# Top-k attention, convolution gate and phase mixer on one core: bringing 1 / sum to the columns of x by products with the identity

## The chip, the cores and the metric

One NeuronCore of a Trainium2 chip runs the whole program. The metric is the device time in microseconds (us) of that core; a lower time is better. The engines that compute are TensorE (PE; its weight loads have a row of their own, PEld), VectorE (DVE), ScalarE (ACT) and GpSimd (POOL). SyncE (SP) issues most of the DMAs.

## The reference

Three blocks follow each other. The first is attention that keeps the 32 largest scores of a row; the second multiplies a convolution gate by a projection; the third mixes phases over tokens and channels. Cut to what matters here:

```python
scores = scale * np.matmul(q, k.transpose(0, 1, 3, 2))          # batch 4, heads 8, 576 x 576, head size 64
kth = np.partition(scores, -32, axis=-1)[..., -32:-31]
scores = np.where(scores >= kth, scores, -1e9)
attn = np.exp(scores - scores.max(-1, keepdims=True))
attn = attn / (attn.sum(-1, keepdims=True) + 1e-09)              # 1 / sum: what the change is about
x = np.matmul(attn, v)                                           # then (batch, 576, 512)

gate_pre = causal_conv5(x, conv_w);  x = (sigmoid(gate_pre) * (x @ w_val)) @ w_out

theta = x @ w_theta
y = w_tok_r @ (x * cos(theta)) + w_tok_i @ (x * sin(theta));  u = x + y
out = u + np.maximum(u @ w_ch, 0.0)
```

## The kernel before

The 32 heads are 16 units `u` of two heads `j` each, four units to a batch. The 576 queries of a head are tiles of 128 rows; the last 64 rows of both heads share one tile. That gives 9 tiles a unit, 144 in all. A tile belongs to a part `(u, x)`: part 0 holds the first 256 columns of x (4 tiles), part 1 the other 320 (5 tiles). Batch 0 takes all its parts 0 first and then all its parts 1 (`SPLIT`); the other batches go unit by unit.

The main loop (L1321) runs one step `i` per tile and writes out the order of the work by hand. In step `i` the kernel computes the scores of tile `i + 3` on PE (`scores_pe`), takes the scores of tile `i + 2` out of PSUM with ACT (`scores_out`), picks the largest of tile `i` on DVE (`pick`, six MAX8 of L573), masks tile `i - 6` (L656) and turns and copies tile `i - 7` (`turn`, `turn_out`). ACT and DVE keep exactly that order; PE, POOL and SP are ordered by priority, which mostly follows it.

When the last tile of a part has been masked, `close` starts a chain (L690). It is a generator that is advanced twice in a step, before `turn` and at the step's end. Call the step in which it starts T. It adds 1e-9 to the row sums (POOL) and takes the reciprocal `rs` (DVE). The sums stand one to a partition, but x is computed with heads and features on partitions and queries in columns, so 1 / sum has to be brought to columns. Before, this takes two hops: `rows` transposes `rs` on PE, and ACT copies the result to `rT` (4 or 5 rows); then `columns(0)` and `columns(1)` multiply a row of the identity by `rT`, and ACT copies each result into `rb`. Meanwhile the products `px` of probabilities and values (L749) run into one of the four buffers of `ps_m`, the PSUM pool that the other two blocks use too. At last DVE multiplies `px` by `rb` (L767), which frees that buffer.

Small PE work that needs some PSUM columns waits in the list `extras`: `last_rows` of every tile (L672, 128 columns, put first), `rows` (128), `columns` (128 or 192). `scores_pe` fills it into the columns that scores leave free: 256 in the bank of the first 256 scores, 192 in the bank of the other 320. Its ACT copies follow the two evictions of that tile in the next step (`run(follow)`).

The last two blocks are jobs (`front`, `back`) that `work` feeds to PE in each step, up to a planned 4150 ns (`BASE`, L63), in order of batches. `front(b)` is appended behind the multiply L767 of the batch's last unit. `drain(("gate", ...))` (L775) runs jobs at once, without the budget, until the gate tiles of an earlier batch are free; the fifth unit before the current one names that batch.

The heads of a unit are loaded by `load_heads`, split into a high and a low half by ACT (`split_high`, L238) and POOL (`split_low`, L244), and copied to where scores use them by `double`. The tuple `when` (L1228) says in which steps this happens: 9, 8, 7, 6 and 3 steps before the unit's first tile, or 7, 5, 5, 4 and 3 steps before it in batch 0. Unit 4 is the first unit of batch 1; its first tile is tile 36, and the part before it, `(3, 1)`, has its first tile at 31. All the loads land in single buffers (`kl`, `ql`).

Of the kernel before, what the change touches and what calls it, by code (L numbers as in the profile page):

```python
# [11 lines left out]
F32 = mybir.dt.float32  # L12
# [29 lines left out]
SPLIT = (0,)  # L42
# [50 lines left out]
def mixer(ctx, tc, qT, kT, vt, w_val, conv_t, w_out, w_theta, w_tok, w_ch, out, flag):  # L93
    nc = tc.nc
    safe = flag is None
    P = 128
    B, S, DM = vt.shape
    U = qT.shape[0]
    NP = U // B
    H2 = S // 2  # L100
    NF = S // P
    REM = S - NF * P
# [418 lines left out]
    def scores_pe(i):  # L521

        s_psum[i] = []
        for lo, hi in COLS:
# [14 lines left out]
            while extras and extras[0][0] <= 512 - a:  # L539
                c, on_pe = extras.pop(0)  # L540
                follow.append(on_pe(bank[:, a : a + c]))
                a += c
# [147 lines left out]
    def close(part):  # L690
# [7 lines left out]
        rT = wk.tile([5, P], F32, tag="rT", name=f"rT_{u}_{x}")  # L698
# [3 lines left out]
        done = set()  # L702

        def rows(spare):
            nc.tensor.transpose(spare[:n, :P], rs[:, :n], ident)

            def f():
                nc.scalar.copy(rT[:n], spare[:n, :P])
                done.add("rows")
            return f  # L710

        def row(k):
            return ident[:n, k : k + 1].broadcast_to([n, 64])

        def columns(m):


            def on_pe(spare):
                c = P + REM * (m * x)
                for j in range(2):  # L720
                    r = slice(64 * j, 64 * j + 64)
                    nc.tensor.matmul(spare[r, :P], row(2 * j + m), rT[:n], start=True, stop=True,  # L722
                                     skip_group_check=True)
                    if c > P:
                        nc.tensor.matmul(spare[r, P:c], row(4), rT[:n, r], start=True, stop=True,
                                         skip_group_check=True)

                def f():
                    nc.scalar.copy(rb[:, m * P : m * P + c], spare[:, :c])  # L729
                    done.add(m)  # L730
                return f
            return on_pe

        extras.append((P, rows))
        yield
        yield
        asked = "rows" in done
        if asked:
            extras.extend((P + REM * (x * m), columns(m)) for m in range(2))
# [17 lines left out]
        while "rows" not in done:  # L757
            yield
            yield
        if not asked:  # L760
            extras.extend((P + REM * (x * m), columns(m)) for m in range(2))
        yield
        yield
        while 1 not in done:
            yield
            yield
# [610 lines left out]
```

## Time and profile before

| what | before |
|---|---|
| time, median of 3 runs | 872.44 us (871.95 to 874.28) |
| profiled execution: its time, its span | 878.3 us, 876.5 us |
| PE busy | 757.3 us (86%) |
| DVE busy | 725.9 us (83%) |
| ACT busy | 652.3 us (74%) |
| POOL busy | 409.2 us (47%) |
| mean granted TensorE clock | 0.932 |

A profile is one execution. Busy times say how much work an engine has; what delays the end is read from idle times and from what ended them. In a line of a timeline the columns are start, duration, engine, line and operation, the tiles written and read, the shape, how many instructions are merged, and in brackets the idle time before the first of them and who ended it.

### The profile page before, as it was taken

What the parts mean: (1) busy time and instruction counts of PE and PEld (TensorE: products, weight loads), DVE (VectorE), ACT (ScalarE), POOL (GpSimd) and SP (SyncE); (2) the same over time, 40 slices, a digit from 0 to 9 for tenths busy, and PEclk for the clock granted to TensorE, in tenths of its full rate; (3) what the DMA queues carried; (4) which work ended last, traced back from release to release, by engine and by line L of the source; (5) the groups of instructions that cost most, each with busy time, mean ns of one, the idle gap of its engine ahead of it and who ended that gap; (6) DMA issues with size and microseconds to landing.
All of it is one profiled execution on the core that took longest, in us unless ns stands there. A gap on an engine that the chain in (4) does not pass through costs nothing.

```text
span 876.5 us, 15920 instructions
## 1 busy us (share of the span) xinstructions
PE 757.3 (86%) x4526; PEld 575.6 (66%) x4526; DVE 725.9 (83%) x2952; ACT 652.3 (74%) x1591; POOL 409.2 (47%) x435
## 2 busy tenths in 40 slices
PE   4477876947879689989798999999998999999995
PEld 2344554624556358676678577769697776699895
DVE  5999998879999778989999999899988697444522
ACT  5787896878979587687878898798987895445611
POOL 4655555344555324354758634445677233003700
PEclk9996788966899979999899999999999999999998
DMA  5665555613433124324735552132755110042001
GB/s 148 169 183 166 143 141 152 174 48 92 131 92 93 43 67 128 94 55 114 225 112 185 191 163 61 46 94 58 216 135 154 44 67 15 1 155 93 3 1 58
DMA packets 73601, 94.35 MB, mean 108 GB/s; under 512 B 13728, under 2 KB 37152, under 8 KB 73504
## 3 DMA queue, kind: packets, MB, share of 16 engines
q1 hardware_dynamic: 73184, 92.82, 37.6%
q8 instruction: 38, 0.62, 0.3%
q14 instruction: 59, 0.48, 0.2%
q10 hardware_dynamic: 320, 0.43, 0.1%
HBM read 49.96 MB, written 13.11 MB: 72 GB/s over the span
## 4 chain that ended last, share of the span: by engine, by line
PE 41%; DVE 37%; ACT 11%; issue 5%; DMA 2%; POOL 2%; SPq 1%; ACTq 0%; POOLq 0%; DVEq 0%
PE py L1090 8%; DVE cand L573 8%; PE px L749 8%; DVE tops L598 6%; DVE s L656 5%; PE ph L507 4%; PE pval L507 3%; DVE cand L579 3%; PE pt L669 3%; PE py L1109 3%; DVE tops L577 3%; PE px2t L507 3%; DVE gp L804 3%; PE ps L536 2%; PE pth L507 2%
## 5 line engine op out<-in xcount | busy, mean ns | idle before, releaser
L593 POOL TENSOR_TENSOR y<-s,n 128x576 f32<-128x576 f32 x144 | 188.4, 1308 | 199.5 <-DVE tops L598 101.6
L573 DVE MAX8 cand<-s 128x8 f32<-128x96 f32 x864 | 210.8, 245 | 1.4 <-ACT s L550 1.4
L585 ACT ACTIVATE n<-s,tops 128x576 bf16<-128x576 f32 x144 | 112.0, 778 | 50.3 <-DVE tops L577 34.4
L656 DVE SCALAR_TENSOR_TENSOR s<-s,thrs,e 128x576 f32<-128x576 f32 x144 | 137.9, 958 | 5.7 <-ACT e L193 5.7
L669 PE MATMUL pt<-ident,s 128*128 128x128 f32 x576 | 99.0, 296 | 49.3 <-ACT pT L688 34.5
L550 ACT ACTIVATE s<-ps 128x256 f32<-128x256 f32 (+1 forms) x288 | 103.9, 406 | 38.2 <-PE ps L722 15.0
L669 PEld LDWEIGHTS pt<-ident,s 128*128 128x128 f32 x576 | 71.1, 149 | 78.1 <-ACT pT L688 42.6
L1090 PE MATMUL py<-w_tok,z 128*128 128x256 f32 (+1 forms) x432 | 115.6, 410 | 6.9 <-DVE z L949 6.7
L749 PE MATMUL px<-pT,v 128*64 128x256 f32 (+3 forms) x640 | 113.3, 455 | 8.2 <-ACT pT L688 7.2
L598 DVE MAX8 tops<-y 128x8 f32<-128x576 f32 x144 | 108.0, 750 | 11.7 <-POOL y L593 11.7
L193 ACT ACTIVATE e<-s,least 128x576 f32<-128x576 f32 x144 | 110.5, 768 | 1.3 <-DVE s L656 0.9
L536 PE MATMUL ps<-kh_None,q 128*128 128x256 f32 x240 | 96.9, 410 | 5.9 <-ACT rb L729 2.7
L688 ACT COPY pT<-pt 128x512 f32<-128x512 f32 x128 | 73.2, 571 | 29.1 <-PE px L749 14.7
L1090 PEld LDWEIGHTS py<-w_tok,z 128*128 128x128 f32 x432 | 78.4, 191 | 24.8 <-issue 7.3
L749 PEld LDWEIGHTS px<-pT,v 128*64 128x64 f32 (+1 forms) x640 | 46.1, 148 | 58.8 <-issue 30.9
L577 DVE MAX8 tops<-cand 128x8 f32<-128x48 f32 x432 | 82.9, 192 | 0.1
L537 PE MATMUL ps<-kl_None,q 128*128 128x256 f32 x240 | 73.7, 309 | 0.0
L536 PEld LDWEIGHTS ps<-kh_None,q 128*128 128x128 f32 x240 | 48.5, 202 | 26.9 <-ACT s L550 7.5
L536 PE MATMUL ps<-kh,q 128*128 128x256 f32 (+1 forms) x80 | 40.1, 506 | 20.5 <-ACT s L550 11.4
L579 DVE MATCH_REPLACE8 cand<-tops,cand 128x48 f32<-128x48 f32 x288 | 55.3, 192 | 0.0
L804 DVE SCALAR_TENSOR_TENSOR gp<-xT,w_conv,gp 128x576 f32<-128x576 f32 (+2 forms) x60 | 50.1, 836 | 4.7 <-POOL gp L796 4.0
L537 PEld LDWEIGHTS ps<-kl_None,q 128*128 128x128 f32 x240 | 49.1, 205 | 3.4 <-issue 1.6
(208 smaller groups left out, 1695.7 us busy)
## 6 DMA issues: line engine op xcount, KB each, us to landing
kh_None<-kh_None SPq DMA_DIRECT2D x48, 144.0 KB, 2.5
kl_None<-kl_None SPq DMA_DIRECT2D x48, 144.0 KB, 2.6
v<-in_vt_dram SPq DMA_DIRECT2D x20, 256.0 KB, 2.9
out_dram<-x2T SPq DMA_DIRECT2D x16, 256.0 KB, 3.2
w<-ch SPq DMA_DIRECT2D x16, 256.0 KB, 4.3
w<-theta SPq DMA_DIRECT2D x16, 256.0 KB, 5.5
raw_hi<-in_w_tok_dram SPq DMA_DIRECT2D x14, 256.0 KB, 2.9
kh<-kh SPq DMA_DIRECT2D x24, 144.0 KB, 2.4
```

Of the source, the lines that this page charges most:

```text
L193: ins = nc.scalar.activation(out, src, func, **more).ins
L536: nc.tensor.matmul(bank[:, :w], q2, kh[:, lo:hi], start=(j == js[0]), stop=False)
L537: nc.tensor.matmul(bank[:, :w], q2, kl[:, lo:hi], start=False, stop=(j == js[-1]))
L573: nc.vector.max(d["cand"][:, k, 8 * x : 8 * x + 8], s_tiles[i][:, x * SUB : (x + 1) * SUB])
L577: nc.vector.max(top, c)
L585: nc.scalar.activation(n, s_tiles[i], AF.Sign, bias=d["tops"][:, k, KC - 1 : KC], scale=-(1.0 + 2.0 ** -22), accum_out=d["acc"][:, k : k + 1])
L593: nc.gpsimd.tensor_tensor(y, s_tiles[i], d.pop(("n", k)), ALU.mult)
L598: nc.vector.max(d["tops"][:, k, KC:K], d.pop(("y", k)))
L656: nc.vector.scalar_tensor_tensor(p, p, thrs[:, i : i + 1], e.exp, ALU.is_ge, ALU.mult, accum_out=part["sums"][:, e.slot : e.slot + 1])
L669: nc.tensor.transpose(e.pt[:, c, :], p[:, c * P : (c + 1) * P], ident)
L749: nc.tensor.matmul(px[64 * j : 64 * j + 64, :], v[r, c, 64 * j : 64 * j + 64], pT[r, k, :], start=(c == 0), stop=(c == NF), skip_group_che ...
L1090: nc.tensor.matmul(ps, z[:, m * P : (m + 1) * P], W["tok"][:, w, lo:hi], start=(i + k == 0), stop=(i == NF))
```

## The change

1. `rs` is brought to columns in one hop. `blocks` makes four products: the stationary operand is a column of `rs`, broadcast to 64, and the moving operand is the identity. They fill 256 columns of one bank, and one ACT copy takes them to `rb`. For part 1, `rows` makes two more products of 64 rows and 64 columns and one more small copy. The transpose, `rT` and the two copies of `columns` are gone.
2. The chain asks for these products at the end of step T, and multiplies from step T + 3 on.
3. `extras` is no longer taken in order: the bank of the first 256 scores takes only items of more than 128 columns (`blocks`), the other bank all the rest (`last_rows`, `rows`).
4. The steps of `when` for unit 4 become 7, 5, 5, 4 and 3 before its first tile.

```diff
-            while extras and extras[0][0] <= 512 - a:
-                c, on_pe = extras.pop(0)
+            for item in list(extras):
+                c, on_pe = item
+                if c > 512 - a or (lo == 0) != (c > P):
+                    continue
+                extras.remove(item)
                 follow.append(on_pe(bank[:, a : a + c]))
                 a += c
...
+        def blocks(spare):
+            for m in range(2):
+                for j in range(2):
+                    nc.tensor.matmul(spare[64 * j : 64 * j + 64, m * P : m * P + P],
+                                     rs[:, 2 * j + m : 2 * j + m + 1].broadcast_to([P, 64]), ident,
+                                     start=True, stop=True, skip_group_check=True)
+            def f():
+                nc.scalar.copy(rb[:, : 2 * P], spare)
+                spread.add(0)
+            return f
         def rows(spare):
-            nc.tensor.transpose(spare[:n, :P], rs[:, :n], ident)
+            for j in range(2):
+                r = slice(64 * j, 64 * j + 64)
+                nc.tensor.matmul(spare[r, :], rs[r, 4:5].broadcast_to([64, 64]), ident[r, r],
+                                 start=True, stop=True, skip_group_check=True)
             def f():
-                nc.scalar.copy(rT[:n], spare[:n, :P])
-                done.add("rows")
+                nc.scalar.copy(rb[:, 2 * P :], spare)
+                spread.add(1)
             return f
...
-        extras.append((P, rows))
         yield
+        extras.append((2 * P, blocks))
+        if x:
+            extras.append((REM, rows))
         yield
-        asked = "rows" in done
-        if asked:
-            extras.extend((P + REM * (x * m), columns(m)) for m in range(2))
         yield
...
-        while "rows" not in done:
-            yield
-            yield
-        if not asked:
-            extras.extend((P + REM * (x * m), columns(m)) for m in range(2))
         yield
         yield
-        while 1 not in done:
+        while len(spread) <= x:
...
-            when = (i0 - 7, i0 - 5, i0 - 5, i0 - 4, i0 - 3) if split else (i0 - 9, i0 - 8, i0 - 7, i0 - 6, i0 - 3)
+            when = (i0 - 7, i0 - 5, i0 - 5, i0 - 4, i0 - 3) if split or i0 and order[k - 1]["x"] and order[k - 1]["u"] // NP in SPLIT else (i0 - 9, i0 - 8, i0 - 7, i0 - 6, i0 - 3)
```

## Rows read from the trace of the kernel before

**Rows 1.** The page: busy times of the engines, and the chain that ended last.
```profile
PE 757.3 (86%) x4526; PEld 575.6 (66%) x4526; DVE 725.9 (83%) x2952; ACT 652.3 (74%) x1591; POOL 409.2 (47%) x435
PE 41%; DVE 37%; ACT 11%; issue 5%; DMA 2%; POOL 2%; SPq 1%; ACTq 0%; POOLq 0%; DVEq 0%
```
**Rows 2.** Two stretches: length, busy PE, PEld, DVE, ACT, POOL; clock; DMA share, GB/s.
```profile
550.00:600.00 50.00, 50.00 (x305) 35.83 (x304) 45.29 (x204) 40.19 (x99) 24.29 (x21) 1.00 0.24 60
...
750.00:800.00 50.00, 50.00 (x372) 44.40 (x371) 21.56 (x48) 22.04 (x55) 4.51 (x4) 1.00 0.34 109
```
**Rows 3.** Timeline of SP: a value load, then unit 4's key load.
```profile
139.51 0.39 SPq L223 DMA_DIRECT2D v<-in_vt_dram  x1
...
140.57 0.52 SPq L216 DMA_DIRECT2D kl_None<-in_kT_dram  x1
```
**Rows 4.** Timeline of ACT: the split of unit 4's keys.
```profile
144.93 0.67 ACT L238 CAST kh_None<-kl_None 128x576 fp32r<-128x576 f32 x1 [7.46 <-DMA kl_None<-in_kT_dram]
```
**Rows 5.** Timeline of DVE: two masks, and the first angle of batch 0's second half.
```profile
147.79 1.26 DVE L656 SCALAR_TENSOR_TENSOR s<-s,thrs,e 128x576 f32<-128x576 f32 x1 [3.58 <-ACT e L193]
...
153.22 0.82 DVE L656 SCALAR_TENSOR_TENSOR s<-s,thrs,e 128x576 f32<-128x576 f32 x1
...
173.94 0.69 DVE L911 SCALAR_TENSOR_TENSOR z<-z,pth 128x512 f32<-128x512 f32 x1 [4.22 <-ACT z L904]
```
**Rows 6.** Timelines of PE and of ACT: the transposes, and a later copy.
```profile
148.28 1.11 PE L669 MATMUL pt<-ident,s 128*128 128x128 f32 x4 [5.66 <-ACT pT L688]
...
171.36 0.58 ACT L688 COPY pT<-pt 128x512 f32<-128x512 f32 x1 [1.95 <-PE px L749]
```
**Rows 7.** Stretches as in rows 2: after that wait, and on from it.
```profile
148.30:156.30 8.00, 7.55 (x34) 5.64 (x35) 7.93 (x29) 7.71 (x23) 4.69 (x7) 0.51 0.14 35
156.30:175.00 18.70, 18.70 (x95) 12.06 (x93) 14.37 (x64) 14.82 (x41) 7.20 (x8) 1.00 0.74 198
```
**Rows 8.** Timeline of DVE: reciprocal and multiply of part (7, 1).
```profile
401.89 0.18 DVE L701 RECIPROCAL rs<-rs 128x5 f32<-128x5 f32 x1
...
427.97 0.48 DVE L767 TENSOR_TENSOR xT<-px,rb 128x320 f32<-128x320 f32 x1
```
**Rows 9.** Timeline of PE: transposes that waited for a reciprocal.
```profile
485.42 0.27 PE L705 MATMUL ps<-ident,rs 128*4 128x128 f32 x1 [1.15 <-DVE rs L701]
...
617.58 0.27 PE L705 MATMUL ps<-ident,rs 128*4 128x128 f32 x1 [1.22 <-DVE rs L701]
...
661.39 0.37 PE L705 MATMUL ps<-ident,rs 128*4 128x128 f32 x1 [2.75 <-DVE rs L701]
```
**Rows 10.** Timeline of PE: products that waited for a multiply, and the first of back(0).
```profile
474.99 0.56 PE L507 MATMUL px2t<-G,hi 128*128 128x320 f32 x2 [2.59 <-DVE xT L767]
...
310.15 1.19 PE L1090 MATMUL py<-w_tok,z 128*128 128x256 f32 x2 [6.74 <-DVE z L949]
```
**Rows 11.** Groups by shape: count, busy us, mean ns, idle us before and who ended it.
```profile
L550 ACT ACTIVATE s<-ps 128x256 f32<-128x256 f32 x144 | 54.5, 379 | 30.0 <-PE ps L673 12.4 <-PE ps L722 12.2 <-PE ps L705 4.5
L729 ACT COPY rb<-ps 128x128 f32<-128x128 f32 x48 | 11.2, 271 | 7.6 <-PE ps L725 7.4
L708 ACT COPY rT<-ps 4x128 f32<-4x128 f32 x16 | 4.1, 254 | 0.2
...
L722 PE MATMUL ps<-rT,ident 4*64 4x128 f32 x128 | 13.4, 291 | 0.0
L507 PE MATMUL px<-ident,x2T 128*64 128x128 f32 x64 | 4.9, 302 | 1.3 <-DVE z L949 1.3
```
**Rows 12.** The chain that ended last: start, length, what; four and sixteen products.
```profile
560.51 0.36 PE ps L722 x4
...
702.26 1.11 PE px L507 x16
```
**Rows 13.** Timeline of DVE: angles inside two stretches where `drain` ran.
```profile
519.27 1.89 DVE L911 SCALAR_TENSOR_TENSOR gp<-gp,pth 128x512 f32<-128x512 f32 x3 [1.11 <-ACT gp L904]
...
695.19 0.69 DVE L911 SCALAR_TENSOR_TENSOR gp<-gp,pth 128x512 f32<-128x512 f32 x1 [4.60 <-ACT gp L904]
```

More of the change, by code (lines that the diff above doesn't have):

```diff
@@ L697, in close @@
         rs = wk.tile([P, 5], F32, tag="rs", name=f"rs_{u}_{x}", bufs=2)
-        rT = wk.tile([5, P], F32, tag="rT", name=f"rT_{u}_{x}")
         rb = wk.tile([P, S - CUT], F32, tag="rb", name=f"rb_{u}_{x}")
@@ L701, in close @@
         nc.vector.reciprocal(rs[:, :n], rs[:, :n])
-        done = set()
+        spread = set()
+        def blocks(spare):
[8 more added lines that the diff above has]
+            return f
         def rows(spare):
-            nc.tensor.transpose(spare[:n, :P], rs[:, :n], ident)
+            for j in range(2):
+                r = slice(64 * j, 64 * j + 64)
+                nc.tensor.matmul(spare[r, :], rs[r, 4:5].broadcast_to([64, 64]), ident[r, r],
+                                 start=True, stop=True, skip_group_check=True)
             def f():
-                nc.scalar.copy(rT[:n], spare[:n, :P])
-                done.add("rows")
-            return f
[L712 to L732, printed above, removed]
-        extras.append((P, rows))
+                nc.scalar.copy(rb[:, 2 * P :], spare)
+                spread.add(1)
+            return f
         yield
+        extras.append((2 * P, blocks))
+        if x:
+            extras.append((REM, rows))
         yield
-        asked = "rows" in done
-        if asked:
-            extras.extend((P + REM * (x * m), columns(m)) for m in range(2))
         yield
```

## Prediction

> **What bounds the kernel now.** I read the page first: PE is busy 757 of 876.5 us, DVE 726, ACT 652, and the chain that ended last runs over PE for 41%, DVE for 37% and ACT for 11% [rows 1]. No engine is the bound alone, so the next view is the busy time by stretch. Early on, DVE sets the pace; from about 310 us on PE has more jobs than it can do, and it is busy 50.00 of 50.00 us both at 550 and at 750, the second time with DVE down to 21.56 [rows 2]. So what counts is: up to 310 us whatever holds DVE or the start of the jobs, behind that PE's work and PE's idle time. The third view is the timeline of each engine, for the idle times over 1 us.
>
> The largest one that the change touches is at 137 to 148 us. ACT stands 7.46 us in front of the split of unit 4's keys, waiting for their DMA [rows 4]. The load was issued at 140.57 only, behind a value load that SP had to hold until 139.51 [rows 3]; it was asked for nine steps ahead, before the buffer `kl` had been read out by part (3, 1). Behind ACT's wait everything queues: DVE waits 3.58 us for the exponentials [rows 5], PE 5.66 us for the copy that frees its transposes' buffer [rows 6]. In the 8 us after that PE is granted 0.51 of its clock, close to the lower of its two levels, 1.2 of 2.4 GHz; then it is busy all of 18.70 us at full clock to catch up [rows 7], and at 171.36 ACT waits 1.95 us for it [rows 6], which is part of the 4.22 us that DVE waits for an angle at 173.94 [rows 5].
>
> **The change, part by part.** The sum is made in the profiled execution, 878.3 us; the median is 872.44, 0.7% less, and I take the difference over to it unscaled but for that 0.7%.
>
> *Unit 4 asked for later.* The load is now issued in step 29 instead of 27, its split is in step 31 instead of 28. The masks at 147.79 and 153.22 are those of steps 30 and 31 [rows 5]; without the 3.58 us the split, at the end of step 31, comes at about 151 us, and the load, which even now has landed at 144.93 [rows 4], is there. ACT's 7.46 us go. Worth to the end: DVE's 3.58 us, and of the 4.22 us the 1.95 that came from PE catching up [rows 5, 6]: -5.5 us. The halves of unit 4's data are also subtracted on POOL three steps later. That work sits beside the mask at 147.79, which took 1.26 us where the next takes 0.82 [rows 5]. It moves with it, so I count nothing for it. The copies of `double`, six DMAs or more a head, come in steps 32 and 33, two steps later than before for the first head. SP's queue holds value loads of batch 0 and weights ahead of them, PE's scores of tile 36 in step 33 would wait for them, and behind PE its transposes. The copies for the split parts of batch 0 run by the same schedule, so I count nothing. Bounds: 0 (a wait of the same size on PE instead) to -7.8 (3.58 + 4.22).
>
> What a mask does beside POOL is told by the row just named: 1.26 us beside the subtraction, 0.82 without [rows 5]. The Trainium skill says why, on the page "SBUF — State Buffer", section "Who interferes with whom": a VectorE instruction with two SBUF inputs shares its second read interface with GpSimd. By that rule the 0.44 us reappear where the subtraction goes, as counted; without it the sum would be -5.9.
>
> *One hop instead of two.* In a part 1 the order of `extras` cost a step: `rows` came when `columns` of part 0 had not been placed, and both would not fit. Part (7, 1) has its reciprocal at 401.89 and its multiply at 427.97, five steps later [rows 8]; by the code a part 0 takes four. Now both take three, since 256 columns are always free in the first bank, and 128 + 64 exactly fill the 192 in the other. Three effects follow.
>
> (a) *No transpose in step T itself.* PE reached that transpose before DVE had made the reciprocal: 1.15, 1.22 and 2.75 us of idle [rows 9], 5.1 in all, each time in a stretch in which PE then has no other long wait. In the new order the products stand a step later and the reciprocal is long there. But DVE is also nearly full in these stretches, so of the 5.1 I take 3.0; bounds 0 and -5.1.
>
> (b) *`px` is freed earlier.* Its buffer, one of four, is held for steps T + 1 to T + 3 instead of T + 4 or T + 5. PE waited 2.59 us for such a multiply at 474.99 [rows 10], the longest such wait. I take -1.5; bounds 0 and -5.2, twice that row for all the smaller ones.
>
> (c) *Jobs start earlier.* `front` of batch 0's second half is appended one step earlier, and with it the angles on which the first product of `back(0)` waits 6.74 us at 310.15 [rows 10]; the last weight is converted before that, so it moves too. A step earlier is worth up to 4.15 us of jobs (`BASE`) in the PE-bound rest. Half of it, -2.0; bounds 0 and -4.2.
>
> *PE's own work.* Before: one transpose and eight instructions of `columns` a part (two per product), plus four short ones in a part 1. Four of the eight take 0.36 us on the chain [rows 12], 0.09 each. The new products have 128 rows instead of 4 or 5, a shape the trace shows elsewhere: `px<-ident,x2T`, 128 rows, 64 by 128 columns, sixteen in 1.11 us, 0.07 each [rows 11, 12]. So 8 x 0.02 less a part, and the transpose, some 0.1 us when it waits for nothing (about one instruction of `columns`): 0.26 us in each of the 24 parts after batch 0, hence -6; but the 0.02 rests on stretches of different neighbours, so I take the transposes alone, -2.6. Bounds 0 and -6.
>
> *ACT.* Three copies (254, 271, 271 ns) become one of 256 columns, which costs about what an eviction of 256 does, 379 ns [rows 11]; a part 1 has one small copy more. ACT loses 16 x 0.42 + 16 x 0.2 = 10 us of busy time, rather 7 as its copies overlap. ACT holds 11% of the chain [rows 1]: -0.8.
>
> *The banks.* `last_rows` moves behind the second bank's scores in all 144 tiles. The first eviction then waits for no transpose (30.0 us of ACT's idle time are put down to that bank, 12.4 to `last_rows` [rows 11]), and the next scores may start once it has run; the second eviction ends when PE ends, as before. In a part's step all eight products sit in the first bank, so that eviction waits 0.36 us longer and the second finds its data ready. I count zero; bounds -3 and +3.
>
> *The drain.* `drain(("gate", ...))` stands behind the multiply of a part 1 and so moves two steps ahead, while `front(1)` and `front(2)` cannot, as `back` of the batch before fills the queue. The units whose fifth predecessor ends batch 1 and batch 2, 9 and 13, call it near 519 and 695 us. It must now run up to two steps of jobs more at a stroke, 2 x 4.15 us of PE work, with DVE's picks queued behind the angles that DVE must take (L911), and ACT's masks' exponentials behind sines. DVE stood 1.11 us there the first time, 4.60 the second [rows 13]. PE stays busy, and what is done early is not left for the end: I take +3.0, bounds 0 and +16.6.
>
> Sum: -5.5 - 3.0 - 1.5 - 2.0 - 2.6 - 0.8 + 3.0 = -12.4 us, 866 us for the profiled execution and 860.1 for the median.
>
> **The rivals.**
>
> *DVE takes it back.* PE's shorter waits only let it wait for DVE later, since DVE is at 45 of 50 us where PE is at 50 [rows 2]. Then only unit 4 counts: 872.4 - 5.5 = 866.9. For it: both engines are nearly full. Against: at 750 PE alone is full [rows 2].
>
> *The wait moves.* Unit 4's copies come late enough to hold PE's scores in step 33, and DVE after it: the 5.5 us return there, the rest is absorbed: about 872. For it: six DMAs of each head pass through one queue that was late before [rows 3]. Against: they need no buffer that is still in use by then.
>
> *The drain decides* (the slower side). Each of the two drains leaves DVE idle for the whole of the 8.3 us that it takes on, and the attention, not PE, then ends last: 16.6 - 5.5 - 2.6 - 0.8 = +7.7, 880. It decides from about 9 us of added idle time of DVE in the two stretches. For it: DVE already waits 4.60 us in one [rows 13]. Against: in the other it waits 1.11.
>
> *Weight loads show.* A product with 128 rows can't have its weights loaded beside the one before, so each takes its full 0.30 us instead of 0.07 [rows 11, 12]: 8 x 0.23 x 24 = 44 us more on PE, 904. Sixteen such products in 1.11 us [rows 12] leave no room for that. (The Trainium skill, "TensorE: Matmul & The Clock Gate", Part 3, lets a weight load overlap a running product only where their row groups differ, or into the background buffer; the rows decide for the second.)
>
> *It doesn't do what it says.* A `blocks` finds no place in its step, and the multiply stays at T + 4 or later: unit 4 and part of the copies only, 866.
>
> **How the numbers follow.** Forecast 0.50, around 860 (852 to 866); DVE takes it back 0.18; the wait moves 0.13; the drain decides 0.15; weight loads 0.02; not as it says 0.02. About 0.3%, 2.6 us, is what a measurement of this kernel can tell from no change. Faster by more than that: the forecast, and 866.9 and 866 for all but a little of their chance, 0.69. Same: 872, and that rest, 0.14. Slower: 0.17. The gains' bounds together reach -7.8 - 5.1 - 5.2 - 4.2 - 6 - 0.8 = -29, which would need every wait to count in full; -25 is as far as I go, 847. Above, the range takes in 872 and the nearer part of the drain's case: 875.
>
> **What would show it.** In the trace after: no wait of ACT on `kl_None<-in_kT_dram`, DVE's mask of that step without 3.58 us in front, PE's clock full near 150 us. No wait of PE on L701. L767 three steps behind L701 in every part, and fewer waits of PE on it. `back(0)` starting 8 to 11 us earlier than 310. ACT some 7 us less busy. The prediction is wrong if `back(0)` starts early but the time doesn't follow (then DVE or the drains took it: the idle time of DVE in front of L911 tells), or if scores of tile 36 wait for a DMA.

## The result: slower by 1.3%

The changed kernel takes 884.68 us (median of 4 runs, 884.20 to 884.81) against 873.29 us for the kernel before on the same chip (median of 4 runs; the prediction had 872.44 from 3): a ratio of 1.013, 95% interval 1.0113 to 1.0148. The forecast was 860.1 us, with 875 as its upper end; the sign was wrong, and the time lies outside the range.

| | before | after |
|---|---|---|
| median, us | 873.29 | 884.68 |
| profiled execution / its span | 878.3 / 876.5 | 884.2 / 882.4 |
| busy PE / DVE / ACT / POOL | 757 / 726 / 652 / 409 | 755 / 728 / 642 / 419 |

The profiled execution of before lies 5 us above its median, that of after on it, so the two traces laid side by side show less than the loss.

Busy times on the page of after [rows 1]; then the stretches of [rows 2]: length, busy PE, PEld, DVE, ACT, POOL, clock, DMA share, GB/s:

```profile
PE 754.7 (86%) x4494; PEld 578.9 (66%) x4494; DVE 727.6 (82%) x2952; ACT 641.6 (73%) x1541; POOL 419.2 (48%) x435
```
```profile
550.00:600.00 50.00, 45.90 (x268) 33.78 (x268) 44.29 (x191) 36.37 (x90) 21.59 (x18) 0.90 0.26 66
750.00:800.00 50.00, 49.55 (x354) 42.07 (x353) 26.91 (x62) 20.97 (x51) 2.37 (x4) 1.00 0.34 106
```

Where PE was busy 50.00 of 50.00 us it now has breaks, and in the first of the two stretches the clock is granted at 0.90: PE does not end what it had to do sooner, it waits more.

The timelines of ACT and DVE in after, in the order of rows 4, 5, 8, 10 and 13, with two new waits of the multiply L756 ahead of those of rows 8 (start, length, what, idle time before):

```profile
152.33 0.68 ACT L238 CAST kh_None<-kl_None 128x576 fp32r<-128x576 f32 x1
...
147.36 0.81 DVE L659 SCALAR_TENSOR_TENSOR s<-s,thrs,e 128x576 f32<-128x576 f32 x1
...
270.38 0.49 DVE L756 TENSOR_TENSOR xT<-px,rb 128x320 f32<-128x320 f32 x1 [2.40 <-PE px L743]
326.34 0.49 DVE L756 TENSOR_TENSOR xT<-px,rb 128x320 f32<-128x320 f32 x1 [3.23 <-PE px L743]
403.37 0.18 DVE L703 RECIPROCAL rs<-rs 128x5 f32<-128x5 f32 x1
416.25 0.48 DVE L756 TENSOR_TENSOR xT<-px,rb 128x320 f32<-128x320 f32 x1
...
307.87 2.04 PE L1079 MATMUL py<-w_tok,z 128*128 128x256 f32 x4 [6.56 <-DVE z L938]
...
510.39 1.42 DVE L900 SCALAR_TENSOR_TENSOR gp<-gp,pth 128x512 f32<-128x512 f32 x2 [2.16 <-ACT gp L893]
513.90 0.69 DVE L900 SCALAR_TENSOR_TENSOR gp<-gp,pth 128x512 f32<-128x512 f32 x1 [2.09 <-ACT gp L893]
696.83 0.69 DVE L900 SCALAR_TENSOR_TENSOR gp<-gp,pth 128x512 f32<-128x512 f32 x1 [2.60 <-ACT gp L893]
```

What the change says it does is there. ACT's 7.46 us in front of unit 4's keys [rows 4] are gone, and so are DVE's 3.58 [rows 5]. Part (7, 1) has its multiply 12.9 us behind its reciprocal instead of 26.1 [rows 8]. New are DVE's waits for `px` in front of the multiply. `back(0)` begins only 2.3 us earlier than in [rows 10], where 8 to 11 were forecast, although at its tile 54 DVE was 7.4 us ahead of the kernel before.

Groups of after by shape: count, busy us, mean ns, idle us before and who ended it:

```profile
L553 ACT ACTIVATE s<-ps 128x256 f32<-128x256 f32 x144 | 54.7, 380 | 40.3 <-PE ps L676 39.0 <-PE ps L537 0.9
L709 PE MATMUL ps<-ident,rs 128*64 128x128 f32 x256 | 23.6, 311 | 0.0
L756 DVE TENSOR_TENSOR xT<-px,rb 128x320 f32<-128x320 f32 x16 | 7.8, 487 | 13.6 <-PE px L743 12.8 <-ACT rb L725 0.9
L756 DVE TENSOR_TENSOR xT<-px,rb 128x256 f32<-128x256 f32 x16 | 6.7, 420 | 5.5 <-PE px L743 5.5
L900 DVE SCALAR_TENSOR_TENSOR gp<-gp,pth 128x512 f32<-128x512 f32 x14 | 9.6, 687 | 25.3 <-ACT gp L893 25.2
L721 PE MATMUL ps<-ident,rs 64*64 64x64 f32 x64 | 5.3, 242 | 0.0
```

Each of these products leaves two records in the trace, so the four of `blocks` are eight records. A record is as cheap as counted (23.6 / 256 = 0.092 us, 5.3 / 64 = 0.083), and the products wait for no reciprocal, where [rows 9] had 5.1 us. But DVE waits 18.3 us for `px`, 12.2 of them ahead of tile 142, and ACT's first eviction 39.0 us for `last_rows` (L676), where all its waits came to 30.0 [rows 11]. Its second eviction waits less, 0.5 us for 8.3.

**Who sets the pace.** The stretches from the start to DVE's first pick of tile 142, the last but one, then the rest, of before and of after (busy PE, PEld, DVE, ACT, POOL):

```profile
0.00:724.50 724.50, 615.38 (x3558) 451.37 (x3559) 657.70 (x2793) 590.45 (x1459) 374.78 (x408) 0.92 0.43 120
724.50:876.50 152.00, 141.95 (x969) 124.20 (x969) 68.16 (x161) 61.89 (x132) 34.40 (x27) 0.98 0.15 47
```
```profile
0.00:732.30 732.30, 616.09 (x3542) 458.44 (x3544) 659.95 (x2793) 577.86 (x1409) 384.33 (x408) 0.90 0.43 119
732.30:882.40 150.10, 138.62 (x954) 120.46 (x950) 67.65 (x160) 63.70 (x133) 34.88 (x27) 0.98 0.15 47
```

In the first stretch DVE is the busier engine, 657.7 of 724.5 us, against 615.4 for PE, and its idle time grows from 66.8 to 72.4 us. The rest is PE's and hardly moves, here by 1.9 us. So the time is DVE's work up to tile 142, its idle time there, and 150 us of PE behind it. That is the view that the prediction lacked. It is a reading of the trace: no run here made DVE's own work shorter.

### The profile page after: what moved, and what is told of

Same layout as the page of the kernel before. It is cut to its first block, busy times and chain, and to the rows that moved or that the text cites. A ratio compares the mean times of both kernels' runs of the same rounds, so it can differ in the third digit from the quotient of the medians.

```text
span 882.4 us, 15814 instructions
## 1 busy us (share of the span) xinstructions
PE 754.7 (86%) x4494; PEld 578.9 (66%) x4494; DVE 727.6 (82%) x2952; ACT 641.6 (73%) x1541; POOL 419.2 (48%) x435
## 5 line engine op out<-in xcount | busy, mean ns | idle before, releaser
L672 PE MATMUL pt<-ident,s 128*128 128x128 f32 x576 | 104.0, 301 | 50.0 <-ACT pT L691 22.2
L659 DVE SCALAR_TENSOR_TENSOR s<-s,thrs,e 128x576 f32<-128x576 f32 x144 | 131.6, 914 | 1.8 <-ACT e L193 1.8
L553 ACT ACTIVATE s<-ps 128x256 f32<-128x256 f32 (+1 forms) x288 | 101.8, 407 | 40.8 <-PE ps L676 39.0
L672 PEld LDWEIGHTS pt<-ident,s 128*128 128x128 f32 x576 | 72.4, 152 | 83.1 <-ACT pT L691 35.4
L601 DVE MAX8 tops<-y 128x8 f32<-128x576 f32 x144 | 107.8, 749 | 12.9 <-POOL y L596 12.9
L743 PE MATMUL px<-pT,v 128*64 128x256 f32 (+3 forms) x640 | 105.8, 432 | 5.6 <-ACT pT L691 5.6
L536 PE MATMUL ps<-kh_None,q 128*128 128x256 f32 x240 | 91.8, 395 | 10.4 <-ACT s L553 8.7
L743 PEld LDWEIGHTS px<-pT,v 128*64 128x64 f32 (+1 forms) x640 | 43.1, 140 | 51.5 <-issue 23.6
L793 DVE SCALAR_TENSOR_TENSOR gp<-xT,w_conv,gp 128x576 f32<-128x576 f32 (+2 forms) x60 | 53.2, 887 | 3.3 <-POOL gp L785 2.6
L536 PE MATMUL ps<-kh,q 128*128 128x256 f32 (+1 forms) x80 | 38.0, 482 | 20.4 <-ACT s L553 8.8
```

The source lines that it names most:

```text
L536: nc.tensor.matmul(bank[:, :w], q2, kh[:, lo:hi], start=(j == js[0]), stop=False)
L553: evicted[0] = nc.scalar.activation(st[:, lo:hi], bank[:, : hi - lo], AF.Copy, scale=0.125).ins
L601: nc.vector.max(d["tops"][:, k, KC:K], d.pop(("y", k)))
L659: nc.vector.scalar_tensor_tensor(p, p, thrs[:, i : i + 1], e.exp, ALU.is_ge, ALU.mult, accum_out=part["sums"][:, e.slot : e.slot + 1])
L672: nc.tensor.transpose(e.pt[:, c, :], p[:, c * P : (c + 1) * P], ident)
L743: nc.tensor.matmul(px[64 * j : 64 * j + 64, :], v[r, c, 64 * j : 64 * j + 64], pT[r, k, :], start=(c == 0), stop=(c == NF), skip_group_che ...
```

## The experiments

They are numbered in the order in which they ran. All medians are of fresh runs beside the kernel before, which stood at 872.9 to 873.8.

**Runs 1 and 2: the two parts apart.** Run 1 is the kernel before with only the new `when`, run 2 the changed kernel with only the old one.

```diff
-when = (...) if split else (...)
+when = (...) if split or i0 and order[k - 1]["x"] and order[k - 1]["u"] // NP in SPLIT else (...)
```

> The kernel before with only the steps of unit 4's loads changed (7, 5, 5, 4 and 3 steps before its first tile). In the trace of the changed kernel DVE was 7.4 us ahead of the kernel before at step 54, and lost that lead afterwards. If the lead comes from unit 4 and the loss from the rest of the change, this kernel is 5 to 7 us faster than before: 866 to 868. If the lead is lost to whatever limits PE later on, it is within 2 us of before.

> The changed kernel with unit 4's loads as before. If unit 4 is worth 5 to 7 us on its own and its gain is kept, this is 890 to 892. If the gain is lost in the changed kernel because DVE then only waits longer for PE at the multiply, it stays at 884 to 886.

Measured: 868.60 (865.45 to 874.04; ratio 0.9969, 0.9944 to 0.9993) and 889.49 (1.019, 1.0153 to 1.0227). By the medians unit 4 is worth 4.3 us in the old kernel and 4.8 in the new one, near the forecast 5.5. Run 1 varies by 8.6 us, and by its ratio the gain is 2.7 us, so a difference of 2 or 3 us against it is not sure. All the rest together costs 16 us. From here on unit 4 is asked for later in every kernel, and 868.6, called the base, is what they are compared with.

**Runs 3 and 4: is the multiply, or what follows it, too early?** Run 3 holds the multiply of the changed kernel back by a step (its edit is shown), run 4 only what stands behind it.

```diff
+        yield
+        yield
         while len(spread) <= x:
```

> The changed kernel with the multiply in step T + 4 for every part instead of T + 3. Theory 1 (DVE waits at the multiply for px itself, 13.6 us in 7 waits, because PE is a step behind DVE by then): these waits fall under 4 us and the time to 872 to 877. Theory 2 (the drain two steps ahead makes the long steps): only one of the two steps comes back, the waits for px don't matter, 879 to 882. Theory 3 (last_rows in the second bank holds the second eviction): nothing that it rests on changes, 884.

> The changed kernel with the multiply in step T + 3, but what stands behind it (the drain, the gate, the jobs of the batch) held back to the step in which it came before the change: two steps for a part 1, one for a part 0 of batch 0. Theory 1: DVE still waits 13 us for px, 883 to 886. Theory 2: the long steps at 505 and 691 us fall back and the time to 876 to 880. Theory 3: 884.

Measured: 891.00 and 887.24, both above every range given. In run 3 DVE's waits for `px` were gone and the time was 6 us worse, so removing that wait alone is no cure. Holding the gates and drains back gained nothing either: that the drains come early is not what costs.

**Runs 5 and 6: the banks.** Run 5 lets `last_rows` into the first bank again wherever no blocks are pending; run 6 does the reverse to the base, in steps without other extras. The edit of run 5:

```diff
-                if c > 512 - a or (lo == 0) != (c > P):
+                if c > 512 - a or lo == 0 and c <= P and any(d > P for d, _ in extras):
```

> The changed kernel with one condition altered: in a step in which no blocks of products are pending, last_rows may again stand in the first bank, behind the first 256 columns of scores, as in the kernel before; with blocks pending it goes behind the second bank. Multiply, gate and jobs as in the changed kernel. Theory 3 (the place of last_rows costs the time: in the changed kernel it stands in the second bank in all 144 tiles, and 39.0 us of ACT's idle time are put down to it, where before all waits for the transposes behind the first bank were 30.0): 868 to 874, near the run with unit 4 alone (868.6), and the eviction of 256 columns waits for PE as before. Theory 4 (the products of 128 rows themselves and their dependence on the reciprocal): 883 to 887, as the changed kernel's 884.7.

> The kernel before with unit 4 asked for later (868.6) and one more edit: in a step in which nothing but last_rows is pending, it stands behind the second bank's scores instead of the first's; transposes and columns of the reciprocals keep their two steps. Theory 3 (place of last_rows): 878 to 885. Theory 4 (the products): 868.6 within 3 us, no change.

Measured: 878.62 and 872.16. The bank rule costs 6.1 us in the changed kernel and 3.6 in the old one, the second not sure for the spread of the base. Both theories of that time were half right: some 10 us remained.

**Run 7: the products in the old place.** The base with its transposes and two steps, but each product from `rs` and `ident`; of the edit, the product of 128 rows:

```diff
-nc.tensor.matmul(spare[r, :P], row(2 * j + m), rT[:n], ...)
+nc.tensor.matmul(spare[r, :P], rs[:, 2 * j + m : 2 * j + m + 1].broadcast_to([P, 64]), ident, ...)
```

> The kernel before with unit 4 asked for later (868.6), its transposes and its two steps kept, but each product of columns made from the reciprocals and the identity (128 rows) instead of the transposed reciprocals (4 or 5 rows): the same instructions at the same places in another shape. Theory 3 (place of last_rows): 868.6 within 3 us. Theory 4 (the products themselves): 878 to 886, and PE's products there take well over 0.09 us each.

Measured: 877.64, just under what the products' theory had. But the groups say that this is another case than the change. Run 7, then run 16 (below), where the records stand in runs of eight and four:

```profile
L722 PE MATMUL ps<-ident,rs 128*64 128x128 f32 x256 | 34.0, 296 | 0.0
...
L725 PE MATMUL ps<-ident,rs 64*64 64x64 f32 x64 | 10.4, 242 | 0.0
```
```profile
L709 PE MATMUL ps<-ident,rs 128*64 128x128 f32 x256 | 21.0, 285 | 0.0
...
L721 PE MATMUL ps<-ident,rs 64*64 64x64 f32 x64 | 5.3, 242 | 0.0
```

44.4 us against 26.3 for the same products. The base took 27.1 + 4.7 us for its own, so run 7 gives PE 12.6 us more work, and loses 9.0. The means hide where it comes from; PE in run 7, then in the base:

```profile
412.65 0.44 PE L722 MATMUL ps<-ident,rs 128*64 128x128 f32 x4
413.51 0.43 PE L722 MATMUL ps<-ident,rs 128*64 128x128 f32 x2
413.87 0.32 PE L725 MATMUL ps<-ident,rs 64*64 64x64 f32 x2
414.12 0.43 PE L722 MATMUL ps<-ident,rs 128*64 128x128 f32 x2
414.49 0.32 PE L725 MATMUL ps<-ident,rs 64*64 64x64 f32 x2
```
```profile
409.67 0.44 PE L722 MATMUL ps<-rT,ident 5*64 5x128 f32 x4
409.94 0.29 PE L725 MATMUL ps<-rT,ident 5*64 5x64 f32 x4
```

Two products of 128 rows alone take 0.44 us, as about all of 48 of the 64 groups of `columns` do; the base needs 0.43 for the same two. Only in the other 16, the second group of each part 1, the two shapes alternate: 1.30 us here for 0.56 in the base. 16 x 0.74 = 11.8 of the 12.6 us are there. The change has no such group.

**Runs 8, 9 and 12: the old steps for the multiply.** Runs 8 and 9 put the multiply of run 5 and of the change, and all that stands behind it, one step later for a part 0, two for a part 1. That is one too many for the four parts 1 of batch 0, which the kernel before has at T + 4; run 12 is run 8 with those put right. The edit of run 12; runs 8 and 9 have `range(1 + x)`:

```diff
+        for _ in range(2 if x and b not in SPLIT else 1):
+            yield
+            yield
         while len(spread) <= x:
```

> The kernel of the fifth run (products, unit 4 later, last_rows in the first bank where no blocks are pending; 878.6) with the multiply and all that stands behind it one step later for a part 0 and two for a part 1, so in the steps in which the kernel before has them. Theory 5 (what costs the remaining 10 us is that multiply, gates, drains and jobs come in other steps, part 0 by one and part 1 by two, a shift that neither the run with the multiply one step later nor the one with the gate held back reproduced in full): 866 to 871, near unit 4 alone (868.6). Theory 6 (the place of the products themselves on PE and of their copy on ACT costs it): 876 to 881.

> The changed kernel (884.7) with the same delay: multiply and all behind it one step later for a part 0, two for a part 1; last_rows in the second bank always. Theory 5: 870 to 876 (unit 4 alone and 2 to 6 us for the banks). Theory 6: 883 to 888.

> The kernel of the fifth run (products, unit 4 later, last_rows in the first bank where no blocks are pending; 878.6) with every multiply, and all behind it, in exactly the step of the kernel before: one step later for a part 0 and for batch 0, two for the other parts 1 (the eighth run had two for batch 0's parts 1 as well). What is left against unit 4 alone (868.6) is the place of the products, one step behind the reciprocal, the transposes that are gone, and last_rows in 32 steps. Theory 5 (the steps of the multiply cost the time): 866 to 872. Theory 7 (less work on PE and other waits of PE cost it, whichever step the multiply has): 878 to 888, with over 125 us at half clock.

Measured: 888.93, 890.22 and 875.39, the first two above every range given. Two things follow. The early multiply of the change costs 3.2 us (run 5 against run 12) instead of gaining. And four multiplies of batch 0 that come a step late, with what stands behind them, cost 13.5 us (run 8 against run 12). Run 12 lies between its two expectations: products with the old multiply steps are still 6.8 us above the base.

**Runs 10 and 11: PE's clock.** Busy PE times the granted clock gave less work in the changed kernel, but more time at half clock. Both runs add useless products that nothing reads; from the edit of run 11:

```diff
+    def hold(ps, n):
+        for _ in range(n):
+            nc.tensor.matmul(ps[:, :P], ident, ident, start=True, stop=True, skip_group_check=True)
```

> The changed kernel (884.7) and, behind the scores of each of the first 58 tiles, ten products of the identity with 64 columns of itself into columns of PSUM that nothing reads (PE work without any consumer, 0.09 us each at full clock). Theory 7 (where the time goes is PE's clock and PE's breaks: the change takes 9 us of work off PE, counted at full clock, 712.3 to 703.1 against unit 4 alone, but PE stands at half clock for 152 us instead of 108, which makes its busy time 14 us longer, and idles 14 us more): the filler sits in breaks of PE, fewer stretches up to 310 us fall to half clock (97 us now), and the time is 876 to 882 in spite of 58 x 0.9 us of more work. Rival (DVE and ACT alone set the pace there; the half clock is a consequence of the waits that costs nothing by itself): 885 to 892.

> The changed kernel (884.7) and useless products of the identity with itself on PE at five places behind 380 us at which its trace shows PE waiting for another engine and the clock granted at half for 3.4 to 6.8 us just behind: 36 ahead of the first ph of batch 0 (PE idle 1.05 + 4.98 us), 20 ahead of the first pval of batch 1 (3.26), 24 ahead of the first pth of batch 1 (3.90), 13 and 10 ahead of the transposes of tiles 113 and 123 (2.14 and 1.74). They write where the real products then write, so nothing but PE's breaks is filled. Theory 7: the clock stays full there (30.6 us at half clock less, half of that in time), 870 to 879. Rival (what PE loses at half clock is hidden, because the other engines are late anyway): 883 to 887.

Measured: 924.15 and 884.48. Run 10 says little. Its forecast took 0.09 us, the time of a record, for a product, which leaves two, and counted 580 products. In 5 of the 58 tiles there was no room for them; the other 53 left this group:

```profile
L548 PE MATMUL ps<-ident 128*128 128x64 f32 x1060 | 147.1, 303 | 0.0
```

That is 530 products of 0.28 us, 147 us where 52 had been counted, more than PE's breaks there could take. Run 11 is the clean one. The stretch from 310 us to tile 142, in the changed kernel and in run 11:

```profile
310.00:732.30 422.30, 392.99 (x2488) 315.26 (x2489) 379.77 (x1543) 332.08 (x785) 221.85 (x200) 0.94 0.40 115
```
```profile
310.00:733.30 423.30, 404.36 (x2692) 331.15 (x2690) 379.92 (x1536) 330.83 (x784) 223.00 (x200) 0.98 0.40 114
```

PE's breaks are filled and the mean clock rises from 0.94 to 0.98, to what the base has in its stretch. The time does not move: 884.48 for 884.68. So the half clock behind these five waits is a consequence of PE's waits, not the cause of the loss. (The Trainium skill, "TensorE: Matmul & The Clock Gate", section "Why this matters for your kernels", advises against idle gaps of TensorE because the clock falls behind them. The trace agrees on the fall, 0.94 with the gaps and 0.98 with them filled; that filling them pays did not hold here.)

**Runs 13 to 15: half a step, and other banks.** Run 13 is the change with one more `yield` ahead of the multiply. Runs 14 and 15 cut the products into halves, 128 columns behind `last_rows` in the first bank, 128 or 192 in the second, with run 12's steps and with those of the change; of their edit, the place where the products are asked for:

```diff
-        extras.append((2 * P, blocks))
-        if x:
-            extras.append((REM, rows))
+        extras.extend((P + REM * (m * x), block(m)) for m in range(2))
```

> The changed kernel (884.7) with the multiply, and all behind it, half a step later: at the end of step T + 3, behind the scores, instead of in its middle. Theory 8 (DVE paces the kernel until its last tile; the early multiply makes it wait 12.2 us for px on PE): most of that wait goes, nothing else moves by a step, 875 to 881. Rival (the wait only changes its name, as with a whole step's delay, 891.0): 884 to 891.

> The kernel of the twelfth run (products one step behind the reciprocal, every multiply in the step of the kernel before; 875.4) with the products in two halves: 128 columns behind last_rows in the first bank, 128 or 192 in the second, copied by two instructions. So last_rows stands in the first bank in every tile and each eviction waits for four products at most, as in the kernel with two hops. Theory 9 (the banks: eight products ahead of the first eviction, and last_rows ahead of the second, cost the 6.8 us against unit 4 alone, 868.6): 866 to 871. Rival (the products as such, or the transposes that are gone, cost it): 874 to 878.

> The changed kernel (884.7) with the same halves in both banks, the multiply three steps on as in the change. Theory 9: 7 to 13 us less than the change, 872 to 878. By theory 8 it stays 3 us above the run with the same halves and the old multiply steps, because DVE still waits for px. Rival (early multiply gains once the banks are right, as forecast): 860 to 867.

Measured: 887.90, 878.53 and 880.08, the last 4.6 us under the change, outside both ranges given, and 1.6 us above run 14 where theory 8 had 3. Theory 9 falls: with every `last_rows` back in the first bank the 6.8 us of run 12 stay (9.9 here). Theory 8 falls as it was put: half a step of delay makes it worse. What runs 12 and 14 share is the step of the products.

**Runs 16 to 18: the products behind `px`.** In the change they are asked for ahead of `px` and stand ahead of it in PE's queue; `columns` came behind. These three ask for them behind `px`: run 16 is run 12, run 17 run 5 and run 18 the change, each with that one move. The move also brings them a step later, beside the scores of the next tile; no run separates the two.

```diff
         yield
-        extras.append((2 * P, blocks))
-        if x:
-            extras.append((REM, rows))
         yield
         yield
...
                                  start=(c == 0), stop=(c == NF), skip_group_check=True)
+        extras.append((2 * P, blocks))
+        if x:
+            extras.append((REM, rows))
```

> The kernel of the twelfth run (875.4: products, every multiply in the step of the kernel before) with the products asked for behind px instead of two half steps ahead of it, so they stand behind px in PE's order, as the columns of the kernel before do. Theory 10 (products ahead of px hold up px, and ACT's next copy of transposes, and DVE behind it, wait): ACT's waits for px fall from 16.7 to about 10 us, 866 to 871. Rival (the 6.8 us come from the shape of the products or from the missing transposes): 874 to 878.

> The kernel of the fifth run (878.6) with the products behind px and no other delay: the multiply then follows in step T + 4 for every part, a step earlier than in the kernel before for the later parts 1. Theory 10: DVE's and ACT's waits for px both go, 865 to 872. Rival: 875 to 885.

> The changed kernel (884.7) with the products behind px, nothing else; the multiply follows in step T + 4 for every part, as in the run with the multiply a step later (891.0), from which it differs in the products' place alone. Theory 10: 7 to 15 us under that run, 876 to 884, with some 6 us left for last_rows in the second bank. Rival: 888 to 893.

Measured: 868.44 (867.22 to 869.55; ratio 0.9945, 0.9923 to 0.9967), 876.25 and 877.75. Run 16 gives the 6.8 us back: -7.0 against run 12. Run 18 against run 3, which differ in nothing but this place, gives -13.3. So the times of these two are where theory 10 had them. Its number for ACT's waits was not: from run 12 to run 16 they fell from 16.7 to 14.0 us, not to 10. Run 17 missed, and lies in the rival's range: it differs from run 16 in the multiplies of the parts 1 behind batch 0, which come a step earlier, and is 7.8 us slower.

The timelines of PE and ACT show the place at the second part, run 12, then run 16:

```profile
73.27 1.12 PE L709 MATMUL ps<-ident,rs 128*64 128x128 f32 x8
...
75.90 2.80 PE L743 MATMUL px<-pT,v 128*64 128x256 f32 x20
...
78.83 0.59 ACT L691 COPY pT<-pt 128x512 f32<-128x512 f32 x1 [4.93 <-PE px L743]
```
```profile
74.45 2.71 PE L740 MATMUL px<-pT,v 128*64 128x256 f32 x20
...
79.62 0.66 PE L709 MATMUL ps<-ident,rs 128*64 128x128 f32 x8
...
77.28 0.59 ACT L691 COPY pT<-pt 128x512 f32<-128x512 f32 x1 [3.48 <-PE px L740]
```

`pT` has one buffer for the parts 0 and one for the parts 1, and batch 0 has parts of one kind one behind the other, so there ACT's copy of the next tile's transposes waits until `px` has read it, and behind ACT's copy stand its evictions, which DVE picks from. Four products (eight records) ahead of `px`, 1.12 us at a granted clock of 0.50, make ACT wait 1.45 us longer, and DVE is 1.3 us behind from the next step on. Two more such places, near 99 and 169 us, cost 0.7 and 1.4 us. That is about half of the 7 us: in run 12 DVE is 3.8 us behind run 16 at its tile 54 and 7.4 at tile 142, and neither trace has a wait of ACT for `px` behind 207 us. A part of the rest is in DVE's own busy time; the stretches up to tile 142 of run 12 and run 16:

```profile
0.00:721.60 721.60, 602.29 (x3534) 447.75 (x3536) 660.34 (x2792) 584.74 (x1417) 373.82 (x408) 0.93 0.43 121
```
```profile
0.00:714.20 714.20, 600.15 (x3531) 445.04 (x3532) 655.54 (x2792) 583.16 (x1416) 375.66 (x408) 0.94 0.44 122
```

DVE is busy 4.8 us less for the same 2792 instructions and idle 2.6 us less. What makes DVE's instructions longer is not shown.

## Why the prediction was wrong

**Unit 4** was right: -5.5 forecast, -4.3 and -4.8 measured by the medians, by the waits that were named.

**The step that failed first: what PE saves was counted as time.** The prediction set PE's work and PE's waits as the bound from 310 us on. In run 16 all that was counted there is done: no transpose is left to wait for a reciprocal, PE is busy 741.9 us for the base's 750.0, ACT 644.6 for 652.2. The time is that of the base, 868.44 for 868.60. (a), PE's own work and ACT, -6.4 us in the sum, are worth nothing that can be measured; run 16 still has `last_rows` behind the second bank beside the products, and no run has them behind `px` without that. [Rows 2] had the hint: at 550 us PE was busy 50.00 us, but DVE 45.29, and with jobs to fill PE's time a full PE is no proof of a bound. For this part the rival *DVE takes it back*, 866.9, was right. It does not follow that PE's work is free: 12.6 us more of it, in the groups that evictions wait for, cost 9.0 us in run 7.

**The step that failed worst: the new products' own place.** The text says that they "stand a step later and the reciprocal is long there", and prices what left that place. It never asked what they were moved past. They moved ahead of `px`: +7.0 us (run 12 against 16), +13.3 with the new banks (run 3 against 18), and the change with this one move, which also puts its multiply a step later, is 6.9 us faster (run 18). That the place costs this is shown. How, only in part: ACT's longer waits for `px` bring 3.8 us at most of the 7.4 by which the two traces differ at tile 142, and in the change itself, with the multiply early too, these waits come to 8.2 us, less than the 14.7 of the kernel before.

**The early multiply**, (b) and (c), forecast -3.5 together: +3.2 (run 5 against 12), and +7.8 for the later parts 1 alone with the products behind `px` (run 17 against 16). PE has not ended `px` when DVE comes for it: 18.3 us of waits in the change, where the kernel before had none; [rows 8] shows one of its multiplies. From run 12 to run 5 such waits grow by 11.5 us up to tile 142, while DVE's waits for `py` and `pval` shrink by 8.7: the wait in large part changes its place. Behind `px` the wait is for the copy of `rb` instead; the multiplies of run 17, then run 16:

```profile
L756 DVE TENSOR_TENSOR xT<-px,rb 128x256 f32<-128x256 f32 (+1 forms) x32 | 14.4, 450 | 7.6 <-ACT rb L725 4.7 <-ACT rb L714 2.7 <-ACT n L588 0.3
```
```profile
L759 DVE TENSOR_TENSOR xT<-px,rb 128x256 f32<-128x256 f32 (+1 forms) x32 | 14.4, 448 | 2.6 <-ACT rb L714 2.2 <-PE ps L537 0.3 <-ACT rb L725 0.2
```

**The banks**, 0 with bounds of 3: +6.1 (the change against run 5), +3.6 (run 6), and +1.3 and +1.5, not clear of noise, where the multiply comes later (run 9 against 8, 18 against 17). The step that failed is "The first eviction then waits for no transpose". PE and ACT in the change, then in the kernel before:

```profile
394.46 0.29 PE L537 MATMUL ps<-kl_None,q 128*128 128x256 f32 x1
...
395.10 0.27 PE L676 MATMUL ps<-ident,s 128*64 128x128 f32 x1
...
395.41 0.71 ACT L553 ACTIVATE s<-ps 128x256 f32<-128x256 f32 x2 [2.49 <-PE ps L676]
```
```profile
405.01 0.43 PE L722 MATMUL ps<-rT,ident 4*64 4x128 f32 x4
405.37 0.41 PE L536 MATMUL ps<-kh_None,q 128*128 128x320 f32 x1
...
405.49 0.38 ACT L550 ACTIVATE s<-ps 128x256 f32<-128x256 f32 x1 [2.23 <-PE ps L722]
```

Before, the first eviction starts when the first bank is done, while PE is still at the second. In the change it waits, with the scores of its own bank done at 394.75, until `last_rows` of the second bank ends at 395.37. So do all its waits for L676: 32 of them, with 22.3 us between the end of the first bank's scores and the eviction. In the kernel before no such wait goes past the first bank, and 8.2 us lie behind its scores. How this becomes 6.1 us is open: no wait of DVE for an eviction shows in the change, and run 16, as fast as the base, still has 14.6 us of it.

**The drain**, +3.0: DVE's waits for the angles `gp` up to tile 142 rose from 10.2 to 14.1 us, spread over more and shorter ones than in [rows 13]. The wait has the size that was forecast, but that it costs time is not shown: in run 4 it is down to 8.5 us and the time is no better. The rival *the drain decides* named the right sign and the wrong mechanism.

**Weight loads show** is out: 0.09 us a record, as before. *The wait moves* is out: no scores of tile 36 waited for a DMA.

With what the runs measured, the sum is -4.3 (unit 4) + 0 (one hop) + 7.0 (ahead of `px`) + 3.2 (multiply early) + 6.1 (banks) = +12.0, against 11.4 measured. These are the steps of a path from the base over runs 16, 12 and 5 to the change, so they must add up, and the agreement proves nothing; in another order they have other sizes, as said.

**The mask beside POOL**: 1.26 us [rows 5] became 0.81 once the subtraction had moved, and the loss moved with it, as counted, but grew. DVE's first gate instruction, now beside POOL's subtraction of 1.60 us at 153.09, takes 1.62 us where it took 0.55; it is merged with the one behind it, 0.78 in both. DVE in the kernel before, then in the change:

```profile
163.99 1.36 DVE L804 SCALAR_TENSOR_TENSOR gp<-xT,w_conv,gp 128x320 f32<-128x320 f32 x2
```
```profile
153.42 2.43 DVE L793 SCALAR_TENSOR_TENSOR gp<-xT,w_conv,gp 128x320 f32<-128x320 f32 x2
```

Totals of before, then of after:

```profile
L656 DVE SCALAR_TENSOR_TENSOR s<-s,thrs,e 128x576 f32<-128x576 f32 x144 | 137.9, 958 | 5.7 <-ACT e L193 5.7
...
L613 DVE TENSOR_TENSOR eq<-eq,tops 128x24 f32<-128x24 f32 x48 | 16.9, 353 | 0.0
```
```profile
L659 DVE SCALAR_TENSOR_TENSOR s<-s,thrs,e 128x576 f32<-128x576 f32 x144 | 131.6, 914 | 1.8 <-ACT e L193 1.8
...
L616 DVE TENSOR_TENSOR eq<-eq,tops 128x24 f32<-128x24 f32 x48 | 21.0, 439 | 0.0
```

The masks lose 6.3 us and a small two-input product of DVE gains 4.1, which fits, though more than POOL's place differs between these kernels. The Trainium skill ("SBUF — State Buffer", section "Who interferes with whom") has a DVE instruction with two SBUF inputs contend with a GpSimd instruction that reads SBUF. The trace agrees for the mask and the gate: 0.81 to 1.26 and 0.55 to 1.62 us.

What stays open: how the 7.8 us of run 17 divide between the copies of `rb` (5.0 us more wait), the angles (3.5 more) and DVE's own work (5.1 us more busy up to tile 142); why DVE's busy time for the same instructions differs, by 4.8 us between runs 12 and 16; and by which way the banks and the place of the products delay DVE.

## What to carry to other kernels

Before pricing waits, split the time into the pacing engine's work, its idle time and the tail behind it; an engine that background jobs keep busy need not be the bound. Work taken off PE bought nothing here (run 16), while work added where others wait for it cost 9.0 us (run 7). For an instruction that is moved, write down what it now stands ahead of on its own engine, and who waits for that: four short products asked for ahead of `px` cost 7.0 us here, more than all that the change saved. In a schedule with several tuned distances, move one at a time; run 16, the same products in the old steps behind `px`, is as fast as the best kernel of this study, 0.5% under the kernel before.

## What the hardware showed that was not expected

- A record of the same product, a column of `rs` by the identity, two records a product, took on the mean of a whole execution, stretches at half clock included, 0.082 us in runs of eight behind `px` (run 16), 0.092 in the change, and 0.111 in the shorter runs of run 14 (28.4 us for 256).
- Two products of 128 rows and two of 64 took 1.30 us where the shapes alternate in the trace (run 7). In the base, products of 5 rows in the same place, four records of each shape in a row, took 0.56.
- A product that loads the whole identity, 128 by 128, for only 64 columns took 0.28 us (run 10); one that loads 64 columns of weights for 128 took 0.16 (run 16, two records of 0.082).
- Keeping PE's clock up, 0.98 for 0.94 over some 420 us, bought nothing (run 11).
- With work behind the second bank's scores, ACT's eviction of the first bank starts in this program only when that work is done (32 of 32 waits in the change); no wait of the kernel before does so.
